# Routed mixture at the end of a fused kernel: gathers, fetches and scatters exchange places, and the splits of overflow weights move by halves

## The chip, the cores and the metric

The kernel runs on one core of one Trainium2 chip. The metric is the device time of one execution in microseconds; smaller is better. The engines of a core have lists of their own and meet at semaphores: TensorE (PE, with its weight loads PEld), VectorE (DVE), ScalarE (ACT), GpSimd (POOL) and SyncE (SP, which here only issues DMAs).

## The reference, cut to what matters

Three layers run one after the other: a causal attention with decay, a dense mixture of four experts, and a routed mixture of eight. The change lies in the last, which is, for 1152 rows `x` of 512 numbers:

```python
skip_score = x @ w_skip
do_compute = skip_score > 0
out = x.copy()
xc = x[do_compute]
logits = xc @ w_gate
e_idx = np.argmax(logits, axis=1)
gate_w = probs[np.arange(len(xc)), e_idx]        # probs: softmax of logits
for e in range(E):
    mask = e_idx == e
    h = np.maximum(xc[mask] @ w1[e], 0.0)        # 512 x 1024 a expert
    y[mask] = gate_w[mask, None] * (h @ w2[e])   # 1024 x 512
out[do_compute] = xc + y
```

So a row is sent to at most one expert. All numbers are float32.

## The kernel before

The first 500 us are the attention and the dense mixture; the change leaves them alone. The dense mixture writes its result, which is also the residual of the last layer, to `out` in HBM. Routing gives each row an expert and a rank within it.

The routed mixture runs over ten tiles. Tiles 0 to 7 (class `Few`, one an expert) take the first 64 rows of an expert. Rows beyond these are overflow; tiles 8 and 9 (class `Many`, `k` = 0 and 1) take them in blocks of 128, and which expert a block belongs to is known only at run time. A loop for still more blocks follows and has none to do for this input.

A tile has these parts. `x_in` transposes its gathered rows. `up(0)` and `up(1)` are the first product. For `Few` each covers half of the contraction; for `Many` each gives one half of the hidden width, from a half of the weights of its own, so that `up(0)` reads half 0 and `up(1)` half 1. `turn` transposes the hidden rows on TensorE, and VectorE and ScalarE copy one half of them each, to `ht` (`Few`). `down` is the second product; behind it VectorE adds the residual (L1155, L1220), and `scatter` or `scatter_rows` (L1097, L1106) writes the rows to their places in `out`, an indirect DMA of GpSimd's. Since all scatters write `out` and the gathers read it, each scatter waits until the one before has landed, and a gather and a scatter wait for each other in the order of the code.

`Many` multiplies in parts: `split(a, h)` makes a high part (`wh`, a cast on ScalarE, L1179) and a low part (`wl`, a subtraction on VectorE, L1180) of half `h` of the weights, `a` = 0 for up and 1 for down, in two instructions on each engine. It has to come before the product that reads it.

Weights come in halves of 1 MB through a ring of 17 buffers. Those of tiles 0 to 7 are loaded by SP (`load_m`, L147), each as soon as the buffer is free. Those of tiles 8 and 9 are fetched by GpSimd with an indirect DMA (`fetch`, L1110, called by `load_over`), two a step, because their addresses are computed.

The order of each engine's list is that in which the code is written out. The loop takes step `i`: the first up half of tile `i + 1`, `turn` of tile `i`, `x_in` of tile `i + 2`, the second up half, the splits that the table `ahead` names for this step, `down` of tile `i` with its scatter, two fetches. In step 1 the list of overflow rows is made (`lists`) and the two blocks of 512 numbers a row are gathered (`gather_rows`, L1101); the scatter of tile 0 stands ahead of that, in `tiles[0].down()`.

Of the kernel before, what the change touches and what calls it, by code (L numbers as in the profile page):

```python
# [25 lines left out]
E1, E2, F = 4, 8, 1024  # L26
# [21 lines left out]
def kernel(  # L48
# [47 lines left out]
    idx = const.tile([P, E2], I32, name="idx")  # L96
# [34 lines left out]
    def ring(i):  # L131
        a, e, h = chunks[i]
        pl, tag = mpool[i % RING]
        wm[a, e, h] = pl.tile([P, 4, HF], F32, tag=tag, name=f"wm_{i}")
        return wm[a, e, h], a, e, h
# [93 lines left out]
    with ExitStack() as at:  # L229
# [362 lines left out]
        for n in range(2, len(steps) + LAG_AV):  # L592
# [9 lines left out]
            if n < len(steps):  # L602
                p, i = steps[n]
# [3 lines left out]
            if n >= LAG_AV:  # L607
                p, i = steps[n - LAG_AV]
                for i in AVS.get(i, ()):
                    emit_av(p, i)  # L610
            if n < len(steps):
                p, i = steps[n]
# [31 lines left out]
    xes, xos, ys = [], [], []  # L644
# [17 lines left out]
    with ExitStack() as mo:  # L662
# [334 lines left out]
        h = DM // 2  # L997
# [98 lines left out]
    def scatter(y, ix):  # L1096
        G.indirect_dma_start(out=outr, out_offset=bass.IndirectOffsetOnAxis(ap=ix, axis=0),  # L1097
                             in_=y, in_offset=None, bounds_check=2 * N - 1, oob_is_err=False)

    def gather_rows(x, ix):  # L1100
        G.indirect_dma_start(out=x, out_offset=None, in_=out,  # L1101
                             in_offset=bass.IndirectOffsetOnAxis(ap=ix, axis=0),
                             bounds_check=N - 1, oob_is_err=False)
# [5 lines left out]
    def fetch(w, a, ix):  # L1109
        G.indirect_dma_start(out=w.rearrange("p c f -> p (c f)"), out_offset=None, in_=tables[a],  # L1110
                             in_offset=bass.IndirectOffsetOnAxis(ap=ix, axis=0),
                             bounds_check=2 * E2 * P - 1, oob_is_err=False)

    def load_over(i):
        w, a, e, h = ring(i)
        fetch(w, a, idxw[:, e - E2, h:h + 1])

    class Few:
# [27 lines left out]
        def down(self):  # L1146
            for j in range(4):
                for h in range(2):
                    for g in range(2):
                        T.matmul(out=self.yp[RT * g:RT * g + RT, 0:HD],  # L1150
                                 lhsT=self.ht[:, j * P + RT * h:j * P + RT * h + RT],
                                 rhs=wm[1, self.e, h][:, j, g * HD:(g + 1) * HD], start=(j == 0 and h == 0),
                                 stop=(j == 3 and h == 1))
            y = ys[self.e % 4]
            V.scalar_tensor_tensor(out=y, in0=self.yp[:, 0:HD], scalar=gate[:, self.e:self.e + 1],  # L1155
                                   in1=xes[self.e], op0=ALU.mult, op1=ALU.add)
            scatter(y, idx[:, self.e:self.e + 1])

    class Many:

# [94 lines left out]
    def spread(t0, t1):  # L1255
        for t in range(t0, t1):
            V.tensor_scalar(out=oho[:, t], in0=sloto, scalar1=pos[:, t:t + 1], scalar2=None, op0=ALU.is_equal)
# [9 lines left out]
    def lists():  # L1267
        po = ups[3][:, 0:KO * 5 * E2].rearrange("p (k j e) -> p k j e", k=KO, j=5)
        for t in range(NB):
            for k in range(KO):  # L1270
                T.matmul(out=po[:, k], lhsT=oho[:, t, k, :], rhs=perm[:, t, :, :], start=(t == 0 and k == 0),
                         stop=(t == NB - 1 and k == KO - 1))
        listed(po, KO, idxo, gato)

    tiles = [Few(e) for e in range(E2)] + [Many(k) for k in range(KO)]
# [11 lines left out]
    tiles[2].x_in()  # L1287
    tiles[1].up(1)
    spread(0, NB)
    ahead = {E2 - 3: (0, 0), E2 - 2: (1, 0), E2 - 1: (0, 1), E2: (1, 1)}  # L1290
    behind = [i for i in range(len(chunks)) if chunks[i][1] >= E2]
    for i in range(1, len(tiles)):
        last = i + 1 == len(tiles)
        if last:
            for q in range(2):
                tiles[i].turn(q)
            for q in range(2):
                tiles[i].down(q)
            break
        nxt = tiles[i + 1]  # L1300
        nxt.up(0)
        tiles[i].turn()
        if i == 1:
            lists()
            for k in range(KO):
                gather_rows(xos[k], idxo[:, k:k + 1])
        if i + 2 < len(tiles):
            tiles[i + 2].x_in()
        nxt.up(1)
        if i in ahead:  # L1310
            k, a = ahead[i]
            for h in range(2):
                tiles[E2 + k].split(a, h)
        tiles[i].down()
        for _ in range(2):
            if i >= 2 and behind:
                load_over(behind.pop(0))

    reg = nc.values_load_multi_w_load_instructions(extra, min_val=0, max_val=CO * E2)[1][0]  # L1319
    z = tiles[-1]  # L1320
    z.both = 1
    k = KO - 1
# [85 lines left out]
```

## Time and profile before

| | us |
|---|---|
| median of 3 runs | 611.97 (610.84 to 612.70) |
| the profiled execution, its own time | 612.15 |
| its span, first to last instruction | 610.3 |
| TensorE busy in the span | 591.2 (97%) |
| VectorE, ScalarE, GpSimd busy | 321.3, 262.6, 330.9 |

Times in the rows are counted from the start of the span, so what lies around it is 612.15 − 610.3 = 1.85 us. A busy TensorE is a modelled figure, since matmuls are pipelined; the idle stretches between them and the granted clock are what to look for. A row's releaser is the wait that came last by the profile; where that one had long been done, it was another, often a DMA.

### The profile page before, as it was taken

Reading aid. Unit: us, or ns where it says so; the run is one execution under the profiler, and the core shown is the slowest. Engines: PE = TensorE matmul, PEld = TensorE weight load, DVE = VectorE, ACT = ScalarE, POOL = GpSimd, SP = SyncE. Lnnn points to the kernel's source line nnn. Section 1 sums busy time; section 2 is a strip of 40 time slices with the busy share of each in tenths; the row PEclk is TensorE's granted clock in tenths of the full one; section 3 lists DMA queues with packets and bytes.
Section 4 is the critical chain, followed back from the end, with each engine's and each line's share of the span. In section 5 each row is a group of like instructions: output and inputs, shape, how many; then the busy total and the mean of one; then the engine's idle time right before and its main releaser. Section 6 shows DMA issues by size and latency. Waiting matters only on the chain. (4 is left out here: it accounts for less than half of the span.)

```text
span 610.3 us, 10704 instructions
## 1 busy us (share of the span) xinstructions
PE 591.2 (97%) x3975; PEld 490.7 (80%) x3975; DVE 321.3 (53%) x826; ACT 262.6 (43%) x665; POOL 330.9 (54%) x380
## 2 busy tenths in 40 slices
PE   8999899999999999999999999999999999999795
PEld 6788778998898898898998998998988774454474
DVE  6887877655454454544544544544535665312553
ACT  5677788675153243343343333334333212212561
POOL 4869997799177168168159159249332134222411
PEclk9999999999999999999999999999999999999799
DMA  6786550311112012011011101101429957999810
GB/s 202 230 305 216 190 171 23 139 32 60 51 69 70 1 70 69 2 70 56 13 59 37 45 26 53 61 7 63 156 122 335 371 188 305 419 417 420 324 50 24
DMA packets 19126, 84.22 MB, mean 138 GB/s; under 512 B 2942, under 2 KB 3976, under 8 KB 11904
## 3 DMA queue, kind: packets, MB, share of 16 engines
q1 hardware_dynamic: 16832, 73.19, 32.9%
q0 software_dynamic: 2240, 10.32, 4.4%
q8 instruction: 32, 0.52, 0.3%
q14 instruction: 22, 0.18, 0.1%
HBM read 79.44 MB, written 5.28 MB: 139 GB/s over the span
## 5 line engine op out<-in xcount | busy, mean ns | idle before, releaser
L865 PE MATMUL dn<-w2h,hh 128*128 128x512 f32 x288 | 114.4, 397 | 0.0
L867 PE MATMUL dn<-w2h,hl 128*128 128x512 f32 x288 | 112.5, 391 | 0.0
L866 PE MATMUL dn<-w2l,hh 128*128 128x512 f32 x288 | 112.2, 390 | 0.0
L877 DVE SCALAR_TENSOR_TENSOR acc<-dn,dps,acc 128x512 f32<-128x512 f32 (+1 forms) x64 | 47.4, 742 | 98.4 <-PE dn L867 98.2
L156 POOL TENSOR_TENSOR w2l<-rawd,w2h 128x512 fp32r<-128x512 f32 x32 | 40.5, 1296 | 94.5 <-ACT w2h L201 94.4
L220 PE MATMUL p<-xb_h,w 128*128 128x320 f32 x224 | 69.2, 309 | 0.0
L219 PE MATMUL p<-xb_l,w 128*128 128x320 f32 x224 | 69.2, 309 | 0.0
L218 PE MATMUL p<-xb_h,w 128*128 128x320 f32 x224 | 69.1, 309 | 0.0
L867 PEld LDWEIGHTS dn<-w2h,hl 128*128 128x128 f32 x288 | 54.0, 188 | 11.6
L865 PEld LDWEIGHTS dn<-w2h,hh 128*128 128x128 f32 x288 | 54.1, 188 | 11.2 <-issue 1.4
L866 PEld LDWEIGHTS dn<-w2l,hh 128*128 128x128 f32 x288 | 54.1, 188 | 10.0
L218 PE MATMUL p<-xa,w 128*128 128x256 f32 x218 | 61.3, 281 | 0.0
L220 PE MATMUL p<-xa,w 128*128 128x256 f32 x218 | 61.2, 281 | 0.0
L219 PE MATMUL p<-xa,w 128*128 128x256 f32 x218 | 61.2, 281 | 0.0
L201 ACT CAST w2h<-rawd 128x512 fp32r<-128x512 f32 x32 | 18.3, 621 | 84.7 <-PE dn L867 84.7
L156 POOL TENSOR_TENSOR hl<-m,hh 128x256 fp32r<-128x256 f32 (+1 forms) x32 | 25.9, 808 | 43.5 <-ACT hh L827 43.5
L821 DVE SCALAR_TENSOR_TENSOR hl<-p,hh 128x320 fp32r<-128x320 f32 (+1 forms) x62 | 28.5, 459 | 36.1 <-ACT hh L820 36.1
L156 POOL TENSOR_TENSOR w<-ws,w 128x512 fp32r<-128x512 f32 x32 | 40.7, 1293 | 3.3 <-ACT w L175 3.3
L219 PEld LDWEIGHTS p<-xb_l,w 128*128 128x128 f32 x224 | 42.0, 188 | 0.3
L218 PEld LDWEIGHTS p<-xb_h,w 128*128 128x128 f32 x224 | 42.1, 188 | 0.3
L220 PEld LDWEIGHTS p<-xb_h,w 128*128 128x128 f32 x224 | 42.1, 188 | 0.0
L218 PEld LDWEIGHTS p<-xa,w 128*128 128x128 f32 x218 | 41.3, 190 | 0.3
(292 smaller groups left out, 1332.5 us busy)
## 6 DMA issues: line engine op xcount, KB each, us to landing
wm<-in_m SPq DMA_DIRECT2D x32, 1024.0 KB, 9.6
rawu<-in_w SPq DMA_DIRECT2D x8, 1024.0 KB, 4.8
rawd<-in_w SPq DMA_DIRECT2D x8, 1024.0 KB, 4.8
qk<-in_qk SPq DMA_DIRECT2D x7, 640.0 KB, 5.6
qk<-in_qk SPq DMA_DIRECT2D x7, 576.0 KB, 4.0
bias<-nbd SPq DMA_DIRECT2D x14, 288.0 KB, 6.2
v<-in_v SPq DMA_DIRECT2D x8, 320.0 KB, 3.0
bias<-nbd SPq DMA_DIRECT2D x16, 144.0 KB, 6.0
```

The source lines that it names most:

```text
L156: eng.tensor_tensor(out=out, in0=a, in1=b, op=ALU.subtract)
L201: A.copy(out=ws["d", u][0][:, c, :], in_=wr["d", u][:, c, :])
L218: T.matmul(out=ps, lhsT=wt[:, 0, a, i, :], rhs=xh[:, i, :], start=(i == 0), stop=False)
L219: T.matmul(out=ps, lhsT=wt[:, 0, a, i, :], rhs=xl[:, i, :], start=False, stop=False)
L220: T.matmul(out=ps, lhsT=wt[:, 1, a, i, :], rhs=xh[:, i, :], start=False, stop=(i == 1))
L821: V.scalar_tensor_tensor(out=hl[:, j, cs], in0=c, scalar=0.0, in1=hh[:, j, cs].bitcast(F32), op0=ALU.max, op1=ALU.subtract)
L865: T.matmul(out=ps, lhsT=hh[:, j, ks], rhs=wh[:, j, :], start=(j == 0), stop=False)
L866: T.matmul(out=ps, lhsT=hh[:, j, ks], rhs=wl[:, j, :], start=False, stop=False)
L867: T.matmul(out=ps, lhsT=hl[:, j, ks], rhs=wh[:, j, :], start=False, stop=(j == 3))
L877: V.scalar_tensor_tensor(out=a, in0=ps[:, c0:c1], scalar=pe, in1=a, op0=ALU.mult, op1=ALU.add)
```

## The change

Three things are moved. No instruction is added or removed.

- The scatter of tile 0 leaves `down` and stands in step 1 behind the two gathers of overflow rows.
- The two fetches of a step stand ahead of `down` of the tile, and so ahead of its scatter in GpSimd's list.
- The table `ahead` names single halves, and a point in the step for each: ahead of the second up half of the next tile (`q` = 0) or behind it (`q` = 1). Before, both halves stood together behind it. The halves are spread over steps 5 to 8.

```diff
--- before.py
+++ after.py
@@ -1154,7 +1154,8 @@
             y = ys[self.e % 4]
             V.scalar_tensor_tensor(out=y, in0=self.yp[:, 0:HD], scalar=gate[:, self.e:self.e + 1],
                                    in1=xes[self.e], op0=ALU.mult, op1=ALU.add)
-            scatter(y, idx[:, self.e:self.e + 1])
+            if self.e:
+                scatter(y, idx[:, self.e:self.e + 1])
 
     class Many:
 
@@ -1287,7 +1288,13 @@
     tiles[2].x_in()
     tiles[1].up(1)
     spread(0, NB)
-    ahead = {E2 - 3: (0, 0), E2 - 2: (1, 0), E2 - 1: (0, 1), E2: (1, 1)}
+    ahead = {(E2 - 3, 1): [(0, 0, 0)], (E2 - 2, 1): [(0, 0, 1)], (E2 - 1, 0): [(1, 0, 0)],
+             (E2 - 1, 1): [(1, 0, 1), (0, 1, 0)], (E2, 0): [(0, 1, 1)], (E2, 1): [(1, 1, 0), (1, 1, 1)]}
+
+    def splits(i, q):
+        for k, a, h in ahead.get((i, q), ()):
+            tiles[E2 + k].split(a, h)
+
     behind = [i for i in range(len(chunks)) if chunks[i][1] >= E2]
     for i in range(1, len(tiles)):
         last = i + 1 == len(tiles)
@@ -1304,17 +1311,16 @@
             lists()
             for k in range(KO):
                 gather_rows(xos[k], idxo[:, k:k + 1])
+            scatter(ys[0], idx[:, 0:1])
         if i + 2 < len(tiles):
             tiles[i + 2].x_in()
+        splits(i, 0)
         nxt.up(1)
-        if i in ahead:
-            k, a = ahead[i]
-            for h in range(2):
-                tiles[E2 + k].split(a, h)
-        tiles[i].down()
+        splits(i, 1)
         for _ in range(2):
             if i >= 2 and behind:
                 load_over(behind.pop(0))
+        tiles[i].down()
 
     reg = nc.values_load_multi_w_load_instructions(extra, min_val=0, max_val=CO * E2)[1][0]
     z = tiles[-1]
```

GpSimd's list from step 0 to step 4 of the loop, before (`rows` are gathered for tiles 1 to 7, `rowo` for tiles 8 and 9, `out<-rowo` is a scatter, `wm` is a half of weights):

```order
L640 DMA rows<-out,idx 128x256 x7
L1097 DMA out<-rowo,idx 2304x256
L1101 DMA rowo<-out,idxo 128x512 x2
L1097 DMA out<-rowo,idx 2304x256 x2
L1110 DMA wm_6512<-in_m,idxw 128x2048
L1110 DMA wm_6516<-in_m,idxw 128x2048
L1097 DMA out<-rowo,idx 2304x256
L1110 DMA wm_6558<-in_m,idxw 128x2048
L1110 DMA wm_6562<-in_m,idxw 128x2048
L1097 DMA out<-rowo,idx 2304x256
```

The same place after:

```order
L640 DMA rows<-out,idx 128x256 x7
L1101 DMA rowo<-out,idxo 128x512 x2
L1097 DMA out<-rowo,idx 2304x256 x2
L1110 DMA wm_6492<-in_m,idxw 128x2048
L1110 DMA wm_6496<-in_m,idxw 128x2048
L1097 DMA out<-rowo,idx 2304x256
L1110 DMA wm_6538<-in_m,idxw 128x2048
L1110 DMA wm_6542<-in_m,idxw 128x2048
L1097 DMA out<-rowo,idx 2304x256
```

The first two `rowo` gathers stand ahead of all scatters, and each pair of `wm` fetches stands one scatter further up.

VectorE's list from the first split of step 5 to the residual of tile 7, before (the two figures behind `wl` are `k` and the half; `wl_0_0` and `wl_0_1` come twice, first for the up and then for the down weights; L1155 is a tile's residual, L1143 the `ht` copy, L1172 the low part of a block of rows):

```order
L1180 TENSOR_TENSOR wl_0_0_6631<-wm_6512,wh_0_0_6630 128x1024 x2
L1180 TENSOR_TENSOR wl_0_1_6637<-wm_6516,wh_0_1_6636 128x1024 x2
L1155 SCALAR_TENSOR_TENSOR rowo<-yp_6267,gate,rows 128x256
L1143 COPY ht_6245<-tp 128x256
L1172 TENSOR_TENSOR xtol_6240<-tpx,xtoh_6239 128x512
L1180 TENSOR_TENSOR wl_1_0_6692<-wm_6558,wh_1_0_6691 128x1024 x2
L1180 TENSOR_TENSOR wl_1_1_6698<-wm_6562,wh_1_1_6697 128x1024 x2
L1155 SCALAR_TENSOR_TENSOR rowo<-yp_6266,gate,rows 128x256
L1143 COPY ht_6246<-tp 128x256
```

The same place after (lines are one or two numbers further on):

```order
L1181 TENSOR_TENSOR wl_0_0_6631<-wm_6492,wh_0_0_6630 128x1024 x2
L1155 SCALAR_TENSOR_TENSOR rowo<-yp_6267,gate,rows 128x256
L1143 COPY ht_6245<-tp 128x256
L1173 TENSOR_TENSOR xtol_6240<-tpx,xtoh_6239 128x512
L1181 TENSOR_TENSOR wl_0_1_6686<-wm_6496,wh_0_1_6685 128x1024 x2
L1155 SCALAR_TENSOR_TENSOR rowo<-yp_6266,gate,rows 128x256
L1143 COPY ht_6246<-tp 128x256
L1173 TENSOR_TENSOR xtol_6242<-tpx,xtoh_6241 128x512
L1181 TENSOR_TENSOR wl_1_0_6737<-wm_6538,wh_1_0_6736 128x1024 x2
L1181 TENSOR_TENSOR wl_1_1_6756<-wm_6542,wh_1_1_6755 128x1024 x2
L1181 TENSOR_TENSOR wl_0_0_6762<-wm_6584,wh_0_0_6761 128x1024 x2
```

Half 1 of tile 8's up weights stands behind the `ht` copy and the residual that it stood ahead of, and in step 7 both up halves of tile 9 and one down half of tile 8 stand in a row. ScalarE's casts are moved in the same way.

## Rows read from the trace of the kernel before

**Rows 1.** The page: TensorE's granted clock, in tenths, over 40 slices.
```profile
PEclk9999999999999999999999999999999999999799
```

**Rows 2.** By stretch: length, busy (count) of PE, PEld, DVE, ACT, POOL, clock, DMA, GB/s.
```profile
523.00:564.20 41.20, 41.19 (x280) 20.51 (x278) 6.33 (x13) 7.97 (x17) 9.15 (x9) 1.00 1.01 418
564.20:568.80 4.60, 0.02 (x2) 0.03 (x2) 3.08 (x4) 1.99 (x2) 2.99 (x2) 0.74 0.76 314
568.80:574.60 5.80, 5.80 (x33) 3.21 (x33) 0.98 (x2) 3.24 (x5) 4.13 (x5) 0.62 0.81 278
574.60:604.20 29.60, 29.27 (x154) 22.56 (x152) 18.60 (x22) 14.86 (x20) 3.02 (x3) 1.00 0.25 100
```

**Rows 3.** TensorE in time: start, us, engine, line, operation [idle before, releaser].
```profile
554.20 1.94 PE L1135 MATMUL up<-wm,xt 128*64 128x512 f32 x8
555.96 3.62 PE L1150 MATMUL yp<-wm,ht 128*64 128x256 f32 x32
559.42 1.89 PE L1135 MATMUL up<-wm,xt 128*64 128x512 f32 x8
561.23 0.66 PE L1142 MATMUL tp<-ident,hs 128*128 128x128 f32 x4
...
562.25 1.94 PE L1135 MATMUL up<-wm,xt 128*64 128x512 f32 x8
568.78 5.86 PE L1150 MATMUL yp<-wm,ht 128*64 128x256 f32 x32 [4.58 <-DVE ht L1143]
574.56 0.50 PE L1194 MATMUL up<-wh,xtoh 128*128 128x512 f32 x1
...
581.22 3.67 PE L1150 MATMUL yp<-wm,ht 128*64 128x256 f32 x32
```

**Rows 4.** VectorE in time.
```profile
522.94 0.16 DVE L1263 SCALAR_TENSOR_TENSOR idxo<-found 128x2 int32<-128x2 f32 x1
...
559.20 2.36 DVE L1180 TENSOR_TENSOR wl<-wm,wh 128x1024 fp32r<-128x1024 f32 x2 [4.62 <-PE yp L1150]
565.64 2.36 DVE L1180 TENSOR_TENSOR wl<-wm,wh 128x1024 fp32r<-128x1024 f32 x2 [4.08 <-ACT wh L1179]
...
568.31 0.41 DVE L1143 COPY ht<-tp 128x256 f32<-128x256 f32 x1
...
604.15 0.75 DVE L1220 SCALAR_TENSOR_TENSOR yo<-yp,gato,rowo 128x512 f32<-128x512 f32 x1 [4.51 <-PE yp L1216]
```

**Rows 5.** ScalarE in time.
```profile
564.56 1.99 ACT L1179 CAST wh<-wm 128x1024 fp32r<-128x1024 f32 x2 [4.44 <-PE up L1135]
```

**Rows 6.** GpSimd in time.
```profile
521.79 1.02 POOL L1097 DMA_INDIRECT out<-rowo,idx  x1 [5.94 <-DVE oho L1257]
529.62 1.04 POOL L1101 DMA_INDIRECT rowo<-out,idxo  x1 [6.80 <-DMA out<-rowo,idx]
...
539.48 1.02 POOL L1097 DMA_INDIRECT out<-rowo,idx  x1 [7.51 <-DVE ht L1143]
...
548.19 1.04 POOL L1110 DMA_INDIRECT wm<-in_m,idxw  x1 [0.31 <-issue]
549.54 1.00 POOL L1110 DMA_INDIRECT wm<-in_m,idxw  x1 [0.31 <-issue]
```

**Rows 7.** Single DMA issues, at 549.54, 535.67, 543.51: KB, us to landing.
```profile
wm<-in_m,idxw POOLq DMA_INDIRECT x1, 15.0
...
wm<-in_m SPq DMA_DIRECT2D x1, 1024.0 KB, 20.6
...
wm<-in_m SPq DMA_DIRECT2D x1, 1024.0 KB, 21.9
```

**Rows 8.** SP's queue in 540 to 552, 553 to 563, 562 to 564.5: packets, MB, share.
```profile
q1 hardware_dynamic: 650, 4.74, 95.1%
...
q1 hardware_dynamic: 274, 1.97, 47.6%
...
q1 hardware_dynamic: 35, 0.21, 20.8%
```

## The prediction

> **What bounds the kernel now.** I read the clock line of the page first: a 9 (0.9 or more) in 37 slices, then one 7, then two more 9 [rows 1]. The second view, busy time by stretch, shows why [rows 2]. From 523.0 to 564.2 TensorE is busy 41.19 of 41.20 us. From 564.2 to 568.8 it does 0.02 us of work. From 568.8 to 574.6 it works at a granted clock of 0.62, which is a mixture of its two levels, 1.2 and 2.4 GHz. After that it is busy again, 29.27 of 29.60 us at 1.00. So TensorE sets the end everywhere in the last 90 us but in one place, and a change to the order of the other engines can win only what lies there.
>
> The third view, TensorE's own list in time, gives the size [rows 3]. Step 5 of the loop is undisturbed: the second up half of tile 6 starts at 554.20, the down product of tile 5 at 555.96 (1.76 later), the next up half at 559.42 (3.46 later). Step 6 starts its up half at 562.25, so its down product (tile 6) was due at 564.01. It starts at 568.78, and what follows it at 574.56, 5.78 later.
>
> What it waits for: VectorE's copy of the turned hidden rows of tile 6, `ht`, at 568.31 [rows 4]. Its transposes began at 561.23 [rows 3]. VectorE works through its list in order, and ahead of the copy stand the subtractions of both halves of overflow weights of tile 8, 2.36 us a half [rows 4]. The second half could not start before ScalarE's cast at 564.56 [rows 5]. The profile puts that cast's wait down to the up product, which had ended. The true releaser is a transfer: the second fetch was issued at 549.54 and took 15.0 us, so it landed at 564.5 [rows 6, 7]. It is a fetch that tile 8 does not need before its second up half, and it stopped tile 6.
>
> **The change, part by part.**
>
> *The halves apart.* No instruction is added or taken away: 16 casts, 16 subtractions, 10 scatters and 8 fetches on both sides. In step 5 only half 0 stands in front now, and half 1 stands after the `ht` copy of tile 6. Half 0's subtractions ended at 559.20 + 2.36 = 561.56, while the transposes that began at 561.23 still ran, so the copy now comes right behind its transposes, at about 562, two us before TensorE wants it at 564.01. Step 6 then runs as step 5 did. Terms:
> - the wait: 568.78 − 564.01 = 4.77 us;
> - the clock: the down product and its turnaround take 5.78 us after the idle stretch and 3.46 us when TensorE came from work, so 2.32 us.
>
> Sum 7.09 us. The profiled execution took 612.15 us (0.18 above the median of the three runs), so 612.15 − 7.09 = 605.06.
>
> What is late next? I carried the lists of ScalarE and VectorE forward with the durations of before (a cast of half a tile 1.0 us, half of the 2.36 us for its subtraction) and took as due times TensorE's own list of before, less 7.1 from 574.56 on. Expert-half 1 of tile 8 is cast at 564.9, subtracted by 568.4, and due at 571.2 (cover 2.8 us). Tile 9's halves are ready at 576.0 and 578.6, due at 577.7 and 581.4. The down weights of tile 8 are ready at 581 and 586.2, due 585.3 and 588.0. VectorE then runs without a break from 583.8 to 593.0, since three halves and tile 8's result now follow each other; tile 9's `ht` low part is ready at about 592.5 and due at 593.1. That is the thinnest cover, some 0.5 us; beyond it each us costs one. I book nothing for it.
>
> *The gathers in front of the first scatter.* GpSimd's queue before: scatter 0 at 521.79, gathers when it has landed, 529.62, scatter 1 when they have landed, 539.48 [rows 6]. Now the gathers wait only for their list, which VectorE writes at 522.94 [rows 4], so they go at about 523.4; scatter 0 follows 9.86 later, at 533.2, scatter 1 another 7.83 later, at 541.1. The two spans are those of the rows, exchanged. Scatter 1 thus goes 1.6 us later than before. Nothing but GpSimd's own queue waits for it: TensorE reads the gathered rows only behind the transposes of 561.23 [rows 3], 28 us after their new landing. It costs nothing.
>
> *The fetches in front of the scatter.* The first fetch stood behind scatter 2, at 548.19 [rows 6]; now it stands behind scatter 1, at 541.1 + 1.3 = 542.4, 5.8 us earlier, and the second at 543.7. This takes the second fetch's landing from 564.5 to about 559. With the halves apart this buys nothing more, since the cast stands after other work until 564.9 anyway; either edit alone would remove the stall. Behind the moved fetches stand the scatters: scatter 2 now queues behind 2 MB. Each scatter waits for the one before, and the last result's scatter goes at 598; carried on at the pace of the rows, the chain issues the scatter of tile 7 at 587 and has 4 us to spare before that.
>
> What the early fetches cost is SP's loads, which run until 565. SP alone moved 4.74 MB in 12 us, 0.395 MB/us; beside the fetches 1.97 MB in 10 us, 0.197 [rows 8]. Both queues share from 5.8 us earlier on, about 547 instead of 553, so SP falls 5.8 × 0.198 = 1.15 MB behind and makes that up at 0.197: 5.8 us late. The last load of tile 6 (its second down half, issued at 535.67) landed 20.6 us later, at 556.3 [rows 7]; now 562.1, due at 564.0. That of tile 7 landed 21.9 us after its issue at 543.51, at 565.4 [rows 7]; now 571.2, due at 581.22 − 7.1 = 574.1 [rows 3]. Covered by 1.9 and 2.9 us, with SP's share as the row has it. The bounds of this share: 0.395 (no loss), and the lowest row, 0.21 MB in 2.5 us, 0.084 MB/us [rows 8]. I take 0.197, a row of 10 us in which both queues were full throughout; the low one is SP's last load running out. The Trainium skill (DMA: Bandwidth & Descriptors, section Queues, rings and completion order) says that each DMA engine takes its queues in turn, packet by packet. That speaks against moving a fetch ahead of loads that TensorE waits for; by it SP keeps about half, tile 6's load still lands in time, and the sum stays 605.1. The row of 20.8% is further down than equal turns would allow, so the rule alone does not shut out the third rival below.
>
> **The rivals.**
>
> *A little late.* Either SP's share comes out between 0.14 and 0.18 MB/us and tile 6's load lands 0 to 5 us after 564.0, or the thin cover at 593 or a fetch's landing costs TensorE a short wait. For it: covers of 0.5 and 1.9 us. Against: both queues' rows and the spare time of all other halves. A wait of 1 us leaves 6 of the 7 us (606); one of 3 us also brings part of the low clock back: 7.1 − 3 − 1.2 = 2.9, so 609.
>
> *It does not do what it says.* The stall is a load of SP's after all and not the copy. Against: both loads of tile 6 had landed by 556.3 [rows 7]. Time unchanged, 612.
>
> *Slower: SP's loads starve.* If the fetches, now three pairs in a row with hardly a pause, hold SP at the lowest row, 0.084 MB/us, from 547 on, SP still owes 3.0 MB to tile 6 (6 us at 0.395 and 3.3 us at 0.197, by the old landing at 556.3). GpSimd's four pairs and the scatters between them are 8.7 MB, at 0.418 − 0.084 = 0.33 MB/us [rows 2] some 26 us, to 573; SP gets 2.2 MB in that time, and the other 0.8 MB lands at about 575.5. TensorE then idles 11.5 us instead of 4.8, and the low clock stays: 6.7 us slower, 618.8. It decides at 3.0 MB in 21.8 us (the old start 568.78 less 547), 0.14 MB/us: under that the kernel is slower than before. For: the 2.5 us row. Against: the 10 us row.
>
> **How the numbers follow.** Forecast (no stall, no new one) 0.76; a little late 0.14; no effect 0.03; starved 0.07. A difference under 0.3% (1.8 us) is about what a measurement of this kernel can't tell from none. Faster by more: 0.76 and nearly all of the 0.14, so 0.88; within: 0.05; slower: 0.07. The likeliest case's own range is 603.8 to 606.3 (0.9 us for runs, which spread from 610.84 to 612.70, and the 0.5 us cover). To hold 8 in 10 it is stretched to the better half of the late cases: 603.6 to 608.2. The likeliest is 605.1.
>
> **What would show it.** In the profile after, the clock line has no slice under 0.9 before the last two; TensorE's down product of tile 6 starts 1.8 us after its up half and takes 3.6; the `ht` copy of tile 6 comes within 1 us of its transposes; GpSimd's first fetch is issued at 541 to 544; DMA queue shares are near even from 548 on. The forecast is wrong if TensorE shows an idle stretch of over 1 us between 560 and 600, and the releaser tells which rival: an SP load (late or starved), `ht` low of tile 9 (thin cover), or the `ht` copy of tile 6 again (no effect).

## The result, and the profile after

| | before, us | after, us |
|---|---|---|
| median | 611.69 (4 runs, 610.84 to 612.70) | 605.01 (4 runs, 604.11 to 606.35) |
| the profiled execution | 612.15 | 604.57 |
| its span | 610.3 | 602.9 |
| TensorE busy in the span | 591.2 | 588.6 |

The ratio is 0.9892, 95% interval 0.9867 to 0.9917: 1.1% faster, 6.7 us between the medians. The forecast was 605.1, in a range of 603.6 to 608.2.

The clock line of the page, in tenths over 40 slices, answers to [rows 1]:

```profile
PEclk7899999999999999999999999999999999999998
```

The 7 of slice 38 is gone. Two lower slices stand at the very start, far ahead of the change; what they cost isn't known, and TensorE comes to the tail 0.49 us earlier than in the profile of before all the same (the last up half ahead of tile 6's down product starts at 561.76 instead of 562.25).

Busy time by stretch, with the bounds of [rows 2] moved to the same places of the program (length, busy and count of PE, PEld, DVE, ACT, POOL, then clock, DMA share, GB/s). The middle row is step 6, its last up half and the down product of tile 6:

```profile
523.00:561.76 38.76, 38.76 (x271) 19.87 (x267) 6.72 (x12) 7.46 (x15) 12.32 (x12) 1.00 1.01 419
561.76:567.08 5.32, 5.32 (x42) 2.78 (x41) 2.48 (x4) 3.33 (x5) 0.30 (x1) 1.00 1.02 420
567.08:596.70 29.62, 29.31 (x154) 22.60 (x152) 19.75 (x23) 16.64 (x22) 7.83 (x7) 1.00 0.40 155
```

TensorE is idle for 0.31 us of these three rows, all of it in the last, and none of them is under full clock. Its list in time (start, us, engine, line, operation), against [rows 3]:

```profile
561.76 1.94 PE L1135 MATMUL up<-wm,xt 128*64 128x512 f32 x8
563.53 3.62 PE L1150 MATMUL yp<-wm,ht 128*64 128x256 f32 x32
567.08 0.50 PE L1195 MATMUL up<-wh,xtoh 128*128 128x512 f32 x1
...
573.74 3.67 PE L1150 MATMUL yp<-wm,ht 128*64 128x256 f32 x32
...
592.75 1.09 PE L1217 MATMUL yp<-wh,htl 128*128 128x512 f32 x4
```

The down product of tile 6 starts 1.77 us after its up half (before: 6.53), and the next product follows 3.55 us later (before: 5.78). VectorE in time shows why, against [rows 4]:

```profile
557.31 2.36 DVE L1181 TENSOR_TENSOR wl<-wm,wh 128x1024 fp32r<-128x1024 f32 x2 [3.23 <-ACT wh L1180]
...
561.43 0.42 DVE L1143 COPY ht<-tp 128x256 f32<-128x256 f32 x1 [1.37 <-PE tp L1142]
...
565.39 2.36 DVE L1181 TENSOR_TENSOR wl<-wm,wh 128x1024 fp32r<-128x1024 f32 x2 [1.86 <-ACT wh L1180]
...
590.89 0.68 DVE L1209 TENSOR_TENSOR htl<-tp,hth 128x512 fp32r<-128x512 f32 x1
591.49 0.68 DVE L1209 TENSOR_TENSOR htl<-tpx,hth 128x512 fp32r<-128x512 f32 x1
...
596.67 0.75 DVE L1221 SCALAR_TENSOR_TENSOR yo<-yp,gato,rowo 128x512 f32<-128x512 f32 x1 [4.50 <-PE yp L1217]
```

Tile 6's `ht` copy (L1143) waits for its own transposes alone and runs at 561.43; half 1 of tile 8 is subtracted behind it, at 565.39. GpSimd in time, against [rows 6]: scatter 0, now behind the gathers, and the two fetches of tile 8's up weights.

```profile
532.46 1.02 POOL L1097 DMA_INDIRECT out<-rowo,idx  x1 [7.29 <-issue]
...
540.54 1.04 POOL L1110 DMA_INDIRECT wm<-in_m,idxw  x1 [0.30 <-issue]
541.89 1.00 POOL L1110 DMA_INDIRECT wm<-in_m,idxw  x1 [0.31 <-issue]
```

Single DMA issues, the second fetch and SP's second down halves of tiles 6 and 7, issued at 541.89, 535.17 and 543.01 (KB, us to landing), against [rows 7]:

```profile
wm<-in_m,idxw POOLq DMA_INDIRECT x1, 14.2
...
wm<-in_m SPq DMA_DIRECT2D x1, 1024.0 KB, 26.2
...
wm<-in_m SPq DMA_DIRECT2D x1, 1024.0 KB, 27.4
```

The second fetch lands at 556.1 instead of 564.5; in return SP's loads land later, at 561.4 (TensorE wants it from 563.53) and 570.4 (from 573.74). The DMA queues in 556 to 566 (packets, MB, share of the 16 engines) show how they divide the engines, against [rows 8]:

```profile
q1 hardware_dynamic: 292, 2.11, 51.1%
q0 software_dynamic: 296, 2.07, 49.6%
```

Where the 7.58 us between the two profiled executions went: 0.49 before the changed place, 6.99 between that up half and the last residual of the tail (562.25 to 604.15 before, 561.76 to 596.67 after), −0.08 behind it, 0.18 outside the span. The change is the 6.99: the wait, 6.53 − 1.77 = 4.76, and the slower product behind it, 5.78 − 3.55 = 2.23.

### The profile page after: what moved, and what is told of

It reads as the page before. It is cut to its first block, busy times and chain, and to the rows that moved or that the text cites. A ratio compares the mean times of both kernels' runs of the same rounds, so it can differ in the third digit from the quotient of the medians.

```text
span 602.9 us, 10704 instructions
## 1 busy us (share of the span) xinstructions
PE 588.6 (98%) x3975; PEld 489.5 (81%) x3975; DVE 321.8 (53%) x826; ACT 262.2 (44%) x665; POOL 331.1 (55%) x380
```

## The experiments

Four chips were used: the first had each part of the change alone and the run with 20 added products; the second had the longer VectorE, the sooner fetches, the unaltered changed kernel and more to load; the third had 10 added products, the small packets and the four DMAs of 32 partitions; the fourth had 7 added products. The kernel before took 611.08, 611.35, 608.57 and 608.55 us on them (medians of 15 to 19 runs). The chip of the two profiles above is not on record. Times are compared on one chip only, except where the text says so. Ratios to the kernel before are given as recorded; the quotient of the two medians can differ from them by up to 0.3%.

### One part of the change at a time

**The halves apart, alone.** The table `ahead`, `splits` and its two calls are those of the changed kernel; gathers, fetches and scatters stand as before.

```diff
-        nxt.up(1)
-        if i in ahead:
-            k, a = ahead[i]
-            for h in range(2):
-                tiles[E2 + k].split(a, h)
+        splits(i, 0)
+        nxt.up(1)
+        splits(i, 1)
```

> Only the splits move by halves; gathers, fetches and scatters stand as before. Theory (either edit alone removes the stall): the second fetch still lands at about 564.5, but the cast that waits for it stands behind the ht copy of tile 6, so the down product of tile 6 starts 1.8 us after its up half and TensorE has no idle stretch; 605 (604 to 606.5), like the changed kernel. Rival (the early fetches are needed too, since the second half comes too late for tile 8): tile 8's second up half, due at 570.8, waits; 606 to 609. Rival (the stall is a load of SP's): 612.

Measured: 605.28 (604.37 to 606.01), ratio 0.9896 (0.9872 to 0.9921). VectorE and TensorE in time, with the late fetches (issued at 548.64 and 549.98; the second landed 14.5 us later, at 564.5):

```profile
562.21 0.41 DVE L1143 COPY ht<-tp 128x256 f32<-128x256 f32 x1
```
```profile
562.48 1.94 PE L1135 MATMUL up<-wm,xt 128*64 128x512 f32 x8
564.25 2.11 PE L1150 MATMUL yp<-wm,ht 128*64 128x256 f32 x18
```

So the whole gain comes without any earlier fetch. The half that comes at 564.5 is simply no longer in front of anything that TensorE waits for: between 553 and 591 it has no idle stretch over 0.2 us.

**The fetches ahead, alone.**

```diff
-        tiles[i].down()
         for _ in range(2):
             if i >= 2 and behind:
                 load_over(behind.pop(0))
+        tiles[i].down()
```

> Only the two fetches of a step move ahead of the down product and its scatter; both halves of tile 8's up weights are still split together in step 5 ahead of the ht copy of tile 6. Theory: the second fetch lands at about 556, its cast goes at 558.3, its subtractions end at 562.1, and the ht copy follows the residual at 562.6, ended at 563.0 where TensorE wants it at 563.5: no stall, or one of a few tenths; 605.2 (604.3 to 606.5). Rival (the halves apart are what counts): the copy comes a us or more late and the low clock returns in part; 607 to 610.

Measured: 605.09 (604.22 to 606.10), ratio 0.9896 (0.9870 to 0.9921). VectorE and TensorE in time:

```profile
557.77 4.83 DVE L1180 TENSOR_TENSOR wl<-wm,wh 128x1024 fp32r<-128x1024 f32 x4 [3.23 <-ACT wh L1179]
...
562.92 0.41 DVE L1143 COPY ht<-tp 128x256 f32<-128x256 f32 x1
```
```profile
563.99 3.62 PE L1150 MATMUL yp<-wm,ht 128*64 128x256 f32 x32
```

Both halves still stand in front of the copy, but their data are there, so the four subtractions run through and the copy ends at 563.33, 0.66 us before TensorE starts. Either edit alone removes the stall. Their gains don't add up, since it is one stall: the changed kernel, which has both, stands at a ratio of 0.9892 and, in a later run, 0.9903, beside 0.9896 for each alone.

**The gathers ahead, alone.** They stand in front of scatter 0, as in the changed kernel; splits and fetches as before.

> Only the two gathers of overflow rows move ahead of the first scatter. Theory: costs and gains nothing, since nothing but the queue of GpSimd waits for them; the second weight fetch goes at 549 to 551 as before and the stall at tile 6 stays; 611.7 (610.5 to 613). Rival (the gathers' place starts the fetches earlier, and so is part of the gain): under 609. Rival (scatter 1 goes 1.6 us later and the fetch with it): the stall grows by up to 1.6 us; 613.3.

Measured: 611.98 (610.82 to 613.79), ratio 1.0016 (1.0001 to 1.0031), within 0.3% of no change. TensorE in time still has the stall:

```profile
568.82 5.25 PE L1150 MATMUL yp<-wm,ht 128*64 128x256 f32 x32 [4.26 <-DVE ht L1143]
574.00 0.50 PE L1195 MATMUL up<-wh,xtoh 128*128 128x512 f32 x1
```

The second fetch was issued at 550.61 here (before: 549.54) and landed at 564.5 as before, though it went 1.1 us later. The last up half started at 562.62 here, so the product was due at 564.39 and is 4.43 us late; it takes 5.18 us to the next product, 1.63 more than 3.55. The same stall thus costs 6.06 us in this profile, where the profile of before has 6.99: the clock's part differs from one execution to the next.

### The low clock

**Filling the idle stretch.** Products that nothing reads stand ahead of the down product of tile 6 in the kernel before, first 20, then 10, then 7.

```diff
+        if i == E2 - 2:
+            for n in range(20):
+                o = RT * (n % 2)
+                T.matmul(out=ups[3][o:o + RT, :], lhsT=ident[:, 0:RT], rhs=xos[0], start=True, stop=True)
         tiles[i].down()
```

> The kernel before, with 20 more products on TensorE ahead of the down product of tile 6 (identity by gathered rows, into a PSUM bank that tile 9 overwrites later; nothing reads them), about 4.4 us, to stand in the idle stretch of 4.58 us. The wait stays, only TensorE is not idle in it. Theory (2.3 us of the gain are the clock that falls because TensorE had no work): the granted clock stays 1.00 behind the stretch, the down product takes 3.5 us instead of 5.8; 609.4 (608.5 to 610.5). Rival (the low clock there has another cause): 611.7 or, since the products run past the end of the wait, slower.

Measured: 613.76, ratio 1.0034 (1.0017 to 1.0051). I had the size wrong: one such product is two in the profile and costs 0.43 us, so the 20 took 8.75 us and ran 4 us past the wait. TensorE in time:

```profile
573.62 3.62 PE L1150 MATMUL yp<-wm,ht 128*64 128x256 f32 x32
577.17 0.50 PE L1194 MATMUL up<-wh,xtoh 128*128 128x512 f32 x1
```

The down product takes 3.55 us again, and what follows it stands 2.61 us later than in the profile of before (574.56); with 5.78 us it would be 4.84. TensorE came to tile 6 at 565.03 in this profile, 1.02 us late; without that the two are 1.59 and 3.82. If the clock's part were lost in both kernels, or in neither, the difference would be 3.82 to 4.84. The interval of the ratio is 1.0 to 3.1 us, so on this chip the clock's part is in the median of the kernel before and not in this one's.

> The kernel before with half of the added products of the fourth run (10 instead of 20; 20 took 8.75 us in that run's profile, so 10 take 4.4 us, inside the idle stretch of 4.6 us). The wait for the ht copy stays. Theory: the granted clock stays 1.00, the down product starts at its old place and takes 3.5 us instead of 5.8; 2.3 us faster than before, 609.4 (608.5 to 610.3), ratio 0.9963. Rival (the 2.3 us have another cause than the idle stretch): 611.7.

Measured: 611.19, ratio 1.0067 (1.0033 to 1.0100). TensorE in time, and the same two stretches with the granted clock:

```profile
565.83 4.46 PE L1317 MATMUL up<-rowo,ident 128*64 128x512 f32 x20
570.12 3.62 PE L1150 MATMUL yp<-wm,ht 128*64 128x256 f32 x32
```
```profile
565.80:570.10 4.30, 4.30 (x22) 1.44 (x20) 3.20 (x5) 2.04 (x5) 3.69 (x3) 1.00 0.60 206
570.10:573.70 3.60, 3.60 (x35) 2.18 (x31) 0.87 (x2) 2.23 (x3) 2.67 (x4) 1.00 0.81 319
```

The mechanism is there: with TensorE busy during the wait, the clock stays at 1.00 (2.4 GHz) and the down product takes 3.55 us to the next one, where the profile of before has 5.78 at a granted clock of 0.62. The time is not: on this chip TensorE came to tile 6 at 565.83 instead of 564.01, while the `ht` copy came at 568.59 (before: 568.31), so the products ended 1.1 us after the copy.

> The kernel before with 7 of the added products, 3.06 us, so that they end before the ht copy even where TensorE comes to tile 6 some 1.7 us later, as it did in the profile with 10 products, where the first tile's ht copy was late. Theory (the low clock comes from the idle stretch): the granted clock stays 1.00, the down product of tile 6 starts where the ht copy lets it (568.8) and takes 3.5 us instead of 5.8, so 2.3 us faster than before where before has the low clock, 609.4, ratio 0.996; where before comes late to tile 6 and is idle for some 3 us only, the same as before. Rival (the 2.3 us have another cause): the down product takes 5.8 us, ratio 1.000.

Measured: 611.81, ratio 1.0034 (1.0013 to 1.0055). In its profile TensorE came to tile 6 only at 569.21, after the copy (568.14), so there was no wait to fill and the 3 us were simply added. The lateness comes from far ahead of the change; TensorE in time, the first tile's down product and what follows:

```profile
515.76 5.36 PE L1150 MATMUL yp<-wm,ht 128*64 128x256 f32 x32 [2.75 <-DVE ht L1143]
520.95 1.89 PE L1135 MATMUL up<-wm,xt 128*64 128x512 f32 x8
```

In the profile of before this product starts at 512.25 and the next at 515.76, 3.51 us later. Here it starts 3.51 us later and takes 5.19 us, at a granted clock of 0.59 in 516 to 518; 3.51 + 1.68 make up the 5.2 us by which TensorE is late at tile 6. So the clock behind an idle stretch is paid in this place too.

In the profiles from the first two chips that wait is 0.30 us; on the other two it is 1.74 to 2.75, in four profiles. So the runs with 10 and 7 products don't price the clock in the median, and I have no profile of the kernel before from these chips. The price rests on rows, 5.78 against 3.55 us for the same 32 products, on the run with 20 products, and on the next run.

### The thin cover, and SP's share

**VectorE longer.** The changed kernel, with the last two subtractions done three times (`split_low_again` writes the same low parts twice more).

```diff
         splits(i, 1)
+        if i == E2:
+            tiles[E2 + 1].split_low_again(1, 1)
```

> The changed kernel with the last split's two subtractions (low parts of tile 9's second down half) done three times instead of once: 4 more of 1.14 us, 4.54 us more on VectorE in the stretch that runs without a break up to the low part of tile 9's ht. Theory: that stretch is the thinnest cover of the changed kernel; the prediction had 0.5 us there, the profile after has 1.2 us (low part of the first half ready at 591.57, product due at 592.75); so TensorE waits 4.54 - 1.2 = 3.4 us, and some of the clock is lost behind it; 608.4 to 610.5. By a cover of 0.5: 609.1 to 611. Rival (VectorE's list is not on the path there): 605.

Measured: 610.46 (608.87 to 611.69), beside 605.68 for the unaltered changed kernel on the same chip, so 4.8 us. TensorE in time, and the stretch behind the wait:

```profile
596.69 1.20 PE L1223 MATMUL yp<-wh,htl 128*128 128x512 f32 x4 [3.25 <-DVE htl L1215]
597.73 1.86 PE L1223 MATMUL yp<-wh,hth 128*128 128x512 f32 x4
599.38 1.91 PE L1223 MATMUL yp<-wl,hth 128*128 128x512 f32 x4
```
```profile
596.70:602.30 5.60, 5.54 (x16) 4.07 (x16) 0.56 (x2) 0.00 (x0) 0.60 (x1) 0.70 0.07 25
```

Due 0.93 us after the product of 592.35, at 593.28, the product with `htl` starts at 596.69: 3.41 us late, as 4.54 less a cover of 1.2 gives. The 16 products left then take 5.55 us (to 602.24) instead of 3.88 (592.75 to 596.63 above): the granted clock fell after the idle 3.25 us, and 1.67 us are lost once more. 3.41 + 1.67 is the 4.8 measured, within 0.3. The wait and its clock are both paid for.

**Fetches one step sooner still.**

```diff
-            if i >= 2 and behind:
+            if i >= 1 and behind:
```

> The changed kernel with each pair of fetches one step earlier still (the first pair behind scatter 0). The fetches then wait for their buffers: the first goes at about 535, the second at 539, the next two at 543 and 547. Theory (SP's loads share the engines evenly with the fetches): SP falls up to 1 MB further behind, the second down half of tile 6 lands at 564 to 566 instead of 561.3, due at 563.5; TensorE waits 0.5 to 2.5 us and loses some of its clock; 605.5 to 609. Rival (the fetches take what SP can spare): 605. Rival (SP starves as soon as fetches follow without a pause): over 612.

Measured: 605.55 (605.33 to 608.25), the same as 605.68. The second down half of tile 6, issued at 535.66, took:

```profile
wm<-in_m SPq DMA_DIRECT2D x1, 1024.0 KB, 28.9
```

It landed at 564.6, as forecast, 0.5 us after TensorE had started the product that reads it (564.02). The wait that was forecast with it, 0.5 to 2.5 us, did not come: the product took 0.2 us longer. By this landing the cover of SP's loads is used up: by my estimate a load that came a us later would be waited for.

**The unaltered changed kernel beside these.**

> The changed kernel unaltered, beside the three that alter it: 605 (604 to 606.5), ratio to before 0.987 to 0.992. Theory and rivals alike.

Measured: 605.68 (605.14 to 606.65), ratio 0.9903 (0.9881 to 0.9925).

**More for SP to load.** 0.98 MB ahead of the last five of its loads, in four DMAs, into buffers that nothing reads.

```diff
-    load_m(15, NS + 2)
+    load_m(15, 27)
+    for c in range(4):
+        SY.dma_start(out=idle[c], in_=m1[0, 0][:, c, 0:idle[c].shape[1]])
+    load_m(27, NS + 2)
```

> The changed kernel with 0.98 MB more to load on SP's queue ahead of tile 6's second down half (rows of weights into buffers that nothing reads). Theory (SP has 0.2 MB/us there beside the fetches, and tile 6's load has a cover of 2.2 us in the profile after, 1.9 in the prediction): the load lands 4.7 to 5 us later, at 566, TensorE waits 2.5 to 2.8 us, and behind it some of the 2.3 us of clock is lost; 608 to 610.5. Rival (SP makes it up, or nobody waits for these loads): 605 to 606. Rival (starves): the wait is over 5 us; over 612.

Measured: 614.26 (609.60 to 616.58), ratio to before 1.0031 (1.0004 to 1.0058): 8.6 us slower than the unaltered one and slower than the kernel before. TensorE in time:

```profile
562.83 1.93 PE L1136 MATMUL up<-wm,xt 128*64 128x512 f32 x6 [2.39 <-DMA wm<-in_m]
...
572.26 6.13 PE L1151 MATMUL yp<-wm,ht 128*64 128x256 f32 x28 [3.69 <-DMA wm<-in_m]
```

My expectation was too low: what came is the second rival, with over 6 us of waits and a granted clock of 0.52 behind the second (572.3 to 578.4). The profiled execution, 616.04, lies 1.8 us above the median. The queues in 546 to 550 tell why:

```profile
q0 software_dynamic: 180, 1.34, 80.4%
q1 hardware_dynamic: 179, 0.32, 22.5%
```

The two queues moved the same number of packets, 180 and 179, but SP's were of 1.8 KB (its rows here are of 2 KB or less) and the fetches' of 7.4 KB. The share of bytes went by the size of the packets: 0.08 MB/us for SP, the bound that the prediction had for the starved case. SP's list was held as well: from 530.40 on each of its last eight DMAs was issued within 0.1 us of the landing of the one eight places before it, so tile 6's second down half went at 543.42 instead of 535.66. SP's queue had loads under way all that time, so I put the late landing down to the bytes and the share and not to this hold; that was not tried apart. In the changed kernel both have rows of 8 KB, 292 and 296 packets in 10 us above, and so equal bytes. That is what the Trainium skill says in DMA: Bandwidth & Descriptors, section Queues, rings and completion order, of turns packet by packet; the trace agrees, with these counts. The page counts some 9 to 17 descriptors to a packet, where the counts here are of the profile's packets, of one row at most.

**The same bytes in smaller packets.** No byte is added; only the last four loads, down halves of tiles 6 and 7, go as four DMAs of 512 columns each.

```diff
-                eng.dma_start(out=w, in_=(m1, m2)[a][e, h])
+                for c in range(4) if i >= 28 else (slice(0, 4),):
+                    eng.dma_start(out=w[:, c], in_=(m1, m2)[a][e, h][:, c])
```

> The changed kernel, with the last four loads of SP (both down halves of tiles 6 and 7) issued as four DMAs of 256 KB each, one per 512 columns, so that each packet is 2 KB instead of 8 KB; the same bytes into the same buffers. Theory (both queues take turns packet by packet, so the share goes by the packet's size: in the run with more to load, SP's 2 KB packets moved 81 GB/s beside 334 of the fetches' 8 KB packets): from 552 on SP gets 0.08 MB/us whenever fetches are under way, tile 6's second down half lands at 566 to 577, TensorE waits 3 to 13 us and loses the clock behind it; 609 to 619, about 614. This is the rival of the prediction in which SP starves. Rival (the share does not go by the packet's size): 605.

Measured: 609.81 (608.19 to 611.32), ratio to before 1.0018 (0.9994 to 1.0042): no faster than the kernel before on this chip, on which the unaltered changed kernel was not timed. The queues in 566 to 574, and TensorE in time:

```profile
q0 software_dynamic: 393, 2.60, 78.9%
q1 hardware_dynamic: 398, 0.72, 23.9%
```
```profile
565.40 2.33 PE L1151 MATMUL yp<-wm,ht 128*64 128x256 f32 x20
568.79 1.08 PE L1151 MATMUL yp<-wm,ht 128*64 128x256 f32 x8 [1.06 <-DMA wm<-in_m]
571.07 0.65 PE L1151 MATMUL yp<-wm,ht 128*64 128x256 f32 x4 [1.20 <-DMA wm<-in_m]
```

Again equal packets, 393 and 398, and 0.09 MB/us for SP. TensorE waits for the last two of the four pieces, 2.3 us in all, less than the 3 to 13 forecast, because the product starts on the first pieces while the others are under way. Another 1.9 us of this run is the late start of the tail on this chip (565.40 against 563.53), so the time alone would overstate what the packets cost: 605.68 on the second chip, plus 1.9 and 2.3, is 609.9.

**Four DMAs with 8 KB packets,** one per 32 partitions.

```diff
+                n = 4 if i >= 28 else 1
+                for c in range(n):
+                    ps = slice(c * P // n, (c + 1) * P // n)
+                    eng.dma_start(out=w[ps], in_=(m1, m2)[a][e, h][ps])
```

> The same four loads of the changed kernel, again as four DMAs of 256 KB each, but one per 32 partitions, so that the packets stay 8 KB. Theory (packet size sets the share, not the number of DMAs): SP keeps half, tile 6's second down half lands at about 561 as in the changed kernel, no wait; 605 (604 to 606.5). Rival (more DMAs, or fewer partitions in each, slow SP's loads): 607 to 619 as in the run with small packets.

Measured: 619.67 (618.29 to 622.78), ratio 1.0209 (1.0163 to 1.0255). The theory's number was missed by 15 us, by something that I had not thought of. About 4 us of it are the late start on this chip (tile 6's product starts at 568.17, against 564.02 in the unaltered run); that product had no wait, as forecast, and most of the rest is the wait for tile 7's load and the clock behind it:

```profile
585.24 5.78 PE L1153 MATMUL yp<-wm,ht 128*64 128x256 f32 x28 [6.20 <-DMA wm<-in_m]
```

All queues in 556 to 566, then the two of them, and the only one under way in 547 to 550:

```profile
DMA packets 392, 2.56 MB, mean 256 GB/s; under 512 B 80, under 2 KB 80, under 8 KB 80
...
q0 software_dynamic: 194, 1.46, 60.6%
q1 hardware_dynamic: 198, 1.10, 42.0%
...
q1 hardware_dynamic: 95, 0.54, 99.6%
```

The turns are equal here too (194 and 198 packets, 80 of them under 512 B; by the bytes, 178 and 134 were of 8 KB), but the whole rate fell from 420 GB/s to 256 with all engines busy: each packet took longer, those of the fetches too. So it is no control for the number of DMAs. The last row shows that it doesn't take the fetches: with the divided loads in its queue, SP alone kept the engines busy at 0.18 MB/us, where [rows 8] have 0.395. What makes a load of 32 partitions slow the engines down wasn't tried.

## Why the prediction was right, point by point

- **The bound and the stall.** Right. The stall was one copy behind a subtraction that a late fetch held up; with either end of that chain cut, it is gone.
- **The wait, 4.77 us, and the clock, 2.32 us.** Right: 6.99 measured for 7.09. The turnaround took 3.55 us and not 3.46, which is the missing 0.1. That the clock belongs in the sum is shown by the filled wait (3.55 us at 1.00) and by the longer VectorE (1.67 us lost behind an idle 3.25); in the medians the run with 20 products bears it out. The size of this term is that of one profile: with the gathers ahead the same stall cost 1.63 us of clock and 6.06 in all, and the gains in the medians of the later runs, 5.7 to 6.0 us, are nearer to that than to 7.09.
- **The number.** That 605.06 and 605.01 are so close is partly luck. The sum started from an execution 0.46 us above the median of before (612.15 against 611.69) and took off 0.41 us more than the medians differ by (7.09 against 6.68).
- **Either edit alone.** Right, 605.28 and 605.09.
- **The gathers, nothing.** Right, 1.0016. Scatter 0, scatter 1 and the fetches went at 532.5, 539.2 and 540.5, where I had 533.2, 541.1 and 542.4: scatter 0 landed faster in its new place than the row of its old one.
- **SP's loads.** Right: 561.4 and 570.4 against 562.1 and 571.2, covers 2.2 and 3.3 us against 1.9 and 2.9. The share of 0.197 was the right row (0.21 in 556 to 566).
- **The thin cover.** The place was right, the size was not: 1.2 us instead of 0.5. The term that was mis-sized is the moment at which `htl` is ready. I took the second half's (592.17 in the profile after), but the product at 592.75 reads the first half's, ready at 591.57; the second is not read before 595.54.
- **The rival in which SP starves.** It did not happen, and my reason against it was incomplete. I wrote that a share of 20.8% is further down than equal turns allow. Equal turns of packets allow any share of bytes: 22.5% and 23.9% were measured with equal counts of packets. And in that row the counts were not equal: 35 packets beside 151 of the fetches' queue, since it is SP's last load running out. What excluded the rival was that the weights lie in 8 KB rows on both queues, which I had not looked at.
- **The signs.** "No slice under 0.9 before the last two" was put too widely: two slices at the start of the kernel are, far ahead of the change. The first fetch went at 540.54, just ahead of the 541 to 544 that was named.

One thing stays open. On the two chips where the first tile's down product waits some 2 us more, the kernel before is 2.5 us faster than on the others, and one expects the change to win less there: in the kernel before, tile 6 starts when the fetch chain lets it, whether TensorE comes early or late (the `ht` copy at 568.1 to 569.3 in five profiles), and a shorter idle stretch may spare the clock. The rows leave this undecided. The granted clock stayed at 1.00 behind idle stretches of 2.00 us (10 products, first tile) and 2.39 us (more to load); it fell behind 2.69 and 2.75 us (four DMAs of 32 partitions and 7 products, first tile; 0.50 and 0.59 in 516 to 518). The stretch that the 10 products filled would have been some 3 us, from 566.00 to 569.0. So the account is argued and not shown; the changed kernel was not timed on those chips, and why that first wait differs was not found.

## What to carry to other kernels

When an in-order engine holds a step for which the bottleneck waits, look at what stands ahead of it and at the slowest input of that; it is enough to cut one end, by moving the step in front or by fetching earlier, and the gains of the two don't add. Take the clock behind an idle stretch of TensorE into the sum, as a term of its own with its own row. Before a fetch is moved ahead of other loads, compare the row lengths on the two queues: in the runs here shares went by packets, and the queue with the short rows was the one that was late.

## What the runs showed that I had not expected

- Two DMA queues that were both full moved nearly equal counts of packets, whatever the size: 180 and 179, 393 and 398, 296 and 292, 194 and 198, and in the kernel before 231 and 226 (553 to 561). The short packets under 512 B count among them. With 2 KB rows beside 8 KB rows the bytes were 0.32 to 1.34 and 0.72 to 2.60 MB.
- The same megabyte in four DMAs of 32 partitions instead of one of 128 took the total from 420 to 256 GB/s, slowed the other queue's packets as well, and ran at 0.18 MB/us with no other queue beside it.
- SP had at most eight DMAs under way in the run with more to load: eight times in a row the next one went within 0.1 us of the landing of the one eight places before it.
- A product of 64 columns by 512 in float32 counts as two in the profile and takes 0.43 us; I had taken half of that.
